# Fused attention, MLP and gated MLP on one core: weight units taken up one step earlier at the start of the middle stage, and set-up work on GpSimd placed behind the first key maxima

## The chip, the cores and the metric

The kernel runs on one core of one Trainium2 chip. The metric is the device time of one execution in microseconds (us). Five engines work side by side, each through its own list of instructions in order: TensorE (PE; its weight loads are shown as PEld), VectorE (DVE), ScalarE (ACT), GpSimd (POOL) and SyncE (SP), which here issues the DMAs. An engine waits only where an instruction needs another engine's result or a buffer that another engine still reads.

## What is computed

The reference, cut to what matters. Everything is fp32.

```python
def _attn_ref(q, k, v):                      # (2, 8, 768, 64) each
    k_sum = k.reshape(B, H, nb, 32, D).max(axis=3)
    v_sum = v.reshape(B, H, nb, 32, D).mean(axis=3)
    scores_l = scale * q @ k.T                # kept where |i - j| < 16
    scores_s = scale * q @ k_sum.T + np.log(32)
    a = softmax(concat[scores_l, scores_s])
    return a @ concat[v, v_sum]

def _moe_ref(x, w_in, w_out):                 # x (1536, 512), d_ff 2048
    h = x @ w_in
    return (h - np.tanh(h)) @ w_out

def _moe2_ref(x, w1, w2, w3, w_out):          # d_ff 1024
    return ((x @ w1) * (x @ w2)) @ w3 @ w_out
```

The attention output, transposed to (1536, 512), goes through `_moe_ref` and then through `_moe2_ref`.

## The kernel before

**Three stages.** The first stage (to about 125 us) is attention: four query tiles at a time, with masks (`masks`), block maxima of the keys (`key_blocks`), softmax, and block means of the values (`value_blocks`, a matmul with the constant rows in `mean`). Beside it TensorE multiplies `w3` by `wo2` (`w34_part`). The middle stage (125 to about 390 us) is `_moe_ref`; the last one is `_moe2_ref`.

**Split products.** An fp32 product is made of three fp32r matmuls: high by high, low by high, high by low (`split_mm`, L187 to L189). So every operand is needed as a high part (a ScalarE cast) and a low part (a GpSimd subtraction of the high part).

**Weight units.** A weight block of 128x512 comes from memory as 64-bit words (`raw`) and is made into fp32 by hand. This is a unit of the class `Weights`: `start` puts one ScalarE instruction (L109); `unit` puts the three VectorE instructions (L112, L114, L116), after which the `raw` buffer is free and SyncE may load the next block (L93); `high` puts the ScalarE cast to `wh` (L144); `low` puts the GpSimd subtraction to `wl` (L151).

**The middle stage.** A loop over n runs over pairs of a feed-forward block f and a token block k. Step n issues the matmuls `hidden(n)` (12, into `ph`), then the pointwise function `curve`, then the matmuls `back(n - 2)` (12, into `x`). `curve(n, ...)` does two things. It ends step n-1: VectorE's conditional copy (L536), then `high()`: the ScalarE cast to `gh` (L531) and the GpSimd subtraction to `gl` (L192). And it begins step n: ScalarE's `u`, `th`, `sq`, `mk` (L544, L545, L550, L551) and VectorE's L552, L553, L554. `back` of a step needs its `gh` and `gl`.

**What sets the order.** The order on each engine is that in which the program text issues the instructions (a manual schedule). In steps below FIRST = 4 the order is `curve`, `start`, `unit`, cast, and `unit` and the cast are there from step LAG = 2 on; from step 4 on it is `start`, cast, and then `curve` with the unit inside it, right behind the conditional copy:

```python
if n < FIRST:
    cur = curve(n, nxt, cur)
wt.start()
...
if LAG <= n < FIRST:
    wt.unit()
if n >= LAG:
    wt.high()
...
if n >= FIRST:
    cur = curve(n, nxt, cur)
wt.low()
```

**The program's start.** GpSimd makes the identity, the diagonal `band`, the rows of `mean`, the three masks, and only then reaches the copy that puts the first key maxima into the key tile (L316 in `key_blocks(0, 2)`). The first `scores` (L347) need that copy.

Of the kernel before, what the change touches and what calls it, by code (L numbers as in the profile page):

```python
# [7 lines left out]
F32 = mybir.dt.float32  # L8
# [4 lines left out]
ALU = mybir.AluOpType  # L13
# [6 lines left out]
P = 128  # L20
NP = H // 2
BLK, WIN = 32, 16
NB = S // BLK
NBR = 3
QT = 64
# [4 lines left out]
CW = QT + NB  # L30
# [11 lines left out]
LAG = 2  # L42
FIRST = 4
# [13 lines left out]
def fused_kernel(tc, qT, kT, vW, w_in, w_out, w1, w2, w3, wo2, out):  # L57
    nc = tc.nc
# [106 lines left out]
    wt = Weights()  # L165
# [25 lines left out]
    def low_part(eng, out, x, high):  # L191
        eng.tensor_tensor(out=out, in0=x, in1=high.bitcast(F32), op=ALU.subtract)  # L192
# [3 lines left out]
    with tc.tile_pool(name="base", bufs=1) as base, \  # L196
# [12 lines left out]
        for hf in range(2):  # L209
            part = band[hf * QT:(hf + 1) * QT, :]  # L210
            nc.gpsimd.affine_select(out=part, in_=part, pattern=[[1, WK]], compare_op=ALU.is_ge,
                                    fill=NEG, base=-1, channel_multiplier=-1)
            nc.gpsimd.affine_select(out=part, in_=part, pattern=[[-1, WK]], compare_op=ALU.is_ge,
                                    fill=NEG, base=2 * WIN - 1, channel_multiplier=1)

        mean = base.tile([P, 6 + BLK], F32, name="mean")
        nc.gpsimd.memset(mean, 0.0)

        def rows(col, a, b):

            nc.gpsimd.memset(col, 1.0 / BLK)
            for base_, step in ((-a, 1), (b - 1, -1)):
                nc.gpsimd.affine_select(out=col, in_=col, pattern=[[0, 1]], compare_op=ALU.is_ge, fill=0.0,
                                        base=base_, channel_multiplier=step)

        rest = base.tile([P, 1], F32, name="mean_rest")
        rows(mean[:, 6:7], WIN, WIN + BLK)
        rows(mean[:, 7:8], WIN + BLK, QT)
        rows(rest, CW, CW + WIN)
        nc.gpsimd.tensor_tensor(out=mean[:, 7:8], in0=mean[:, 7:8], in1=rest, op=ALU.add)  # L230
        masks = []
        for z in range(3):
            mk = base.tile([P, NC], F32, name=f"mask{z}")
            nc.gpsimd.memset(mk[:, BC], LOG_BLK)
            nc.gpsimd.tensor_copy(out=mk[:, :QT], in_=band[:, :QT])
            nc.gpsimd.tensor_copy(out=mk[:, CW:], in_=band[:, QT:])
            if z == 0:
                nc.gpsimd.memset(mk[:, :WIN], NEG)
            if z == 2:
                nc.gpsimd.memset(mk[:, NC - WIN:], NEG)  # L240
            masks.append(mk)

        w34 = [base.tile([P, DM], F32, tag=f"w34_{i}", name=f"w34_{i}") for i in range(NM)]
        xh = [base.tile([P, KC, TB], F32R, name=f"xh_{k}") for k in range(NTB)]
# [31 lines left out]
        with tc.tile_pool(name="p1", bufs=1) as p1, \  # L276
                tc.tile_pool(name="ps1", bufs=1, space=PSUM) as ps1:
            NG = B * NP * NU
            kt, qt, vg, vrow, st, nm, pr, z = ({} for _ in range(8))
# [19 lines left out]
            def key_blocks(n, z):  # L299

                rows = kt[n]
                chunks = rows[:, :NQ * CW].rearrange("p (t w) -> p t w", w=CW)
                if z < 2:
                    if z == 0:
                        hb[n] = p1.tile([P, 4 * NQ + 2], F32, tag="hb", bufs=2, name=f"hb_{n}")
                    t, w = NQ // 2 * z, 2 * NQ
                    nc.vector.tensor_reduce(
                        out=hb[n][:, w * z:w * (z + 1)], axis=AX.X, op=ALU.max,
                        in_=chunks[:, t:t + NQ // 2, :QT].rearrange("p t (i k) -> p t i k", k=WIN))
                else:  # L310
                    nc.vector.tensor_reduce(out=hb[n][:, 4 * NQ:4 * NQ + 1], in_=rows[:, NQ * CW:NQ * CW + WIN],
                                            axis=AX.X, op=ALU.max)
                    pair = [hb[n][:, i:i + 2 * NB].rearrange("p (n two) -> p n two", two=2)[:, :, 0] for i in (1, 2)]
                    kb = p1.tile([P, NB], F32, tag="kb", bufs=2, name=f"kb_{n}")
                    nc.vector.tensor_tensor(out=kb, in0=pair[0], in1=pair[1], op=ALU.max)
                    nc.gpsimd.tensor_copy(out=chunks[:, :, QT:], in_=kb[:, :].unsqueeze(1).to_broadcast([P, NQ, NB]))  # L316
# [23 lines left out]
            def scores(g):  # L340
                n, u = divmod(g, NU)
                ps = ps1.tile([P, TU, NC], F32, tag="s", bufs=2, name=f"s_{g}")
                for i in range(TU):
                    t = u * TU + i
                    for hf in range(2):
                        r = slice(hf * QT, (hf + 1) * QT)
                        mm(out=ps[r, i, :], lhsT=qt[n][r, t * QT:(t + 1) * QT], rhs=kt[n][r, t * CW:t * CW + NC],  # L347
                           start=True, stop=True)
                st[g] = ps
# [33 lines left out]
            def values(g):  # L383
                n, u = divmod(g, NU)
                sb = st[g]
                av = ps1.tile([P, TU * QT + P], F32, tag="av", bufs=1, name=f"av_{g}")
                for i in range(TU):
                    for hf in range(2):
                        r = slice(hf * QT, (hf + 1) * QT)
                        mm(out=av[r, i * QT:(i + 1) * QT], lhsT=vg[n][:NC, u * TU + i, r], rhs=sb[:, i, r],  # L390
                           start=True, stop=True)
                st[g] = av[:, :TU * QT]
                return av[:, TU * QT:]
# [26 lines left out]
            wt.load(2)  # L420
            for i in range(3):
                key_blocks(0, i)
            scores(0)
            n34 = 0
            NN = B * NP
            for g in range(NG + 4):
                n, u = divmod(g, NU)
# [28 lines left out]
                if 0 <= g - 3 < NG:  # L456
                    rest = values(g - 3)
# [51 lines left out]
        def tmp(tag, n, bufs=2, dt=F32):  # L509
            return p2.tile([P, TB], dt, tag=tag, bufs=bufs, name=f"{tag}_{n}")  # L510
# [8 lines left out]
        def hidden(n):  # L519
            f, k = seq[n][:2]  # L520
            ph = bank(n % 3, f"ph_{n}")
            columns(ph, wt.need(("wi", f)), k)
            if k == NTB - 1:
                wt.release(("wi", f))
            return ph

        def curve(n, ph, prev):

            def high():
                gp[n - 1] = tmp("gh", n, LAG + 1, F32R), tmp("gl", n, LAG + 1, F32R)  # L530
                nc.scalar.copy(out=gp[n - 1][0], in_=g)  # L531
                low_part(nc.gpsimd, gp[n - 1][1], g, gp[n - 1][0][:, :])

            if prev is not None:
                mask, t, g = prev
                nc.vector.copy_predicated(out=g, mask=mask[:, :].bitcast(U32), data=t)  # L536
                if n < FIRST:
                    high()
            if n >= FIRST:
                wt.unit()  # L540
            cur = None
            if ph is not None:
                u, sq, t, mask, gn = (tmp(z, n) for z in ("u", "sq", "th", "mk", "g"))
                nc.scalar.activation(out=u, in_=ph, func=AF.Square)  # L544
                nc.scalar.activation(out=t, in_=ph, func=AF.Tanh)  # L545
                cur = mask, t, gn
            if prev is not None and n >= FIRST:
                high()
            if ph is not None:
                nc.scalar.activation(out=sq, in_=u, func=AF.Square, scale=SS, bias=nsb[:])  # L550
                nc.scalar.activation(out=mask, in_=u, func=AF.Relu, bias=numax[:])  # L551
                nc.vector.tensor_tensor(out=gn, in0=ph, in1=u, op=ALU.mult)  # L552
                nc.vector.tensor_tensor(out=t, in0=ph, in1=t, op=ALU.subtract)  # L553
                nc.vector.scalar_tensor_tensor(out=gn, in0=sq, scalar=GAM, in1=gn, op0=ALU.add, op1=ALU.mult)  # L554
            return cur
# [73 lines left out]
        for n in range(NS + LAG):  # L629
            nxt = hidden(n) if n < NS else None  # L630
            if n == NS:
                a = product_a(0, 0)
            if n == NS + 1:
                pb = half("w2", 0, 0)
                w34_split(0)
            if n < FIRST:
                cur = curve(n, nxt, cur)
            wt.start()
            if n == NS + 1:
                prev = 0, 0, product_b(0, 0, a, pb)  # L640
            if LAG <= n < FIRST:
                wt.unit()
            if n >= LAG:
                wt.high()
            closing = len(evac)
            evacuate()
# [3 lines that stand above are left out]
            if not closing:  # L650
                resplit(2)
            if n >= LAG:
                back(n - LAG)
# [108 lines left out]
        for m in range(1, NM):  # L762
# [7 lines left out]
            a = product_a(m, 0)  # L770
# [122 lines left out]
```

## Time and profile before

| | us |
|---|---|
| median of 3 runs | 583.8 (583.33 to 586.09) |
| the profiled execution, its own time | 583.37 |
| its span, first to last instruction | 581.7 |
| PE busy | 565.4 (97% of the span) |
| DVE busy | 462.1 (79%) |
| ACT busy | 339.1 (58%) |
| POOL busy | 280.8 (48%) |

The span is 1.7 us shorter than the time of the same execution. Busy time says who works, not who is waited for: a PE matmul of 512 columns is shown as 0.39 us long, though the next one begins 0.23 us after it, so gaps of PE show only where one is clearly longer than that. The granted TensorE clock is 1.00 in all the stretches used below (2.4 GHz, the upper of its two levels).

### The profile page before, as it was taken

Reading aid. Unit: us, or ns where it says so; the run is one execution under the profiler, and the core shown is the slowest. Engines: PE = TensorE matmul, PEld = TensorE weight load, DVE = VectorE, ACT = ScalarE, POOL = GpSimd, SP = SyncE. Lnnn points to the kernel's source line nnn. Section 1 sums busy time; section 2 is a strip of 40 time slices with the busy share of each in tenths; the row PEclk is TensorE's granted clock in tenths of the full one; section 3 lists DMA queues with packets and bytes.
Section 4 is the critical chain, followed back from the end, with each engine's and each line's share of the span. In section 5 each row is a group of like instructions: output and inputs, shape, how many; then the busy total and the mean of one; then the engine's idle time right before and its main releaser. Section 6 shows DMA issues by size and latency. Waiting matters only on the chain.

```text
span 581.7 us, 9203 instructions
## 1 busy us (share of the span) xinstructions
PE 565.4 (97%) x3240; PEld 458.3 (79%) x3240; DVE 462.1 (79%) x885; ACT 339.1 (58%) x741; POOL 280.8 (48%) x239
## 2 busy tenths in 40 slices
PE   7889999999999999999999999999999999999997
PEld 5677777777688888888888888888887887888885
DVE  4999897766999999679999978999668587778610
ACT  4889887866789776557767667765324322213110
POOL 4556455543465565225555522557735554616320
PEclk9999999999999999999999999999999999999999
DMA  8998875541323323012323101223000100000021
GB/s 318 349 297 303 307 217 186 154 148 37 98 84 109 110 76 106 0 37 73 109 72 109 37 1 51 93 75 110 0 1 0 72 2 1 1 0 2 1 90 54
DMA packets 18526, 56.56 MB, mean 97 GB/s; under 512 B 1968, under 2 KB 4656, under 8 KB 18480
## 3 DMA queue, kind: packets, MB, share of 16 engines
q1 hardware_dynamic: 18480, 55.98, 28.8%
q8 instruction: 25, 0.41, 0.3%
q14 instruction: 21, 0.17, 0.1%
HBM read 51.64 MB, written 3.15 MB: 94 GB/s over the span
## 4 chain that ended last, share of the span: by engine, by line
PE 73%; DVE 12%; issue 5%; ACT 3%; DMA 3%; POOL 2%; SPq 0%; POOLq 0%; DVEq 0%; ACTq 0%
PE x L188 6%; PE x L187 6%; PE x L189 6%; PE ph L187 6%; PE ph L188 6%; PE ph L189 6%; PE p_w L187 4%; PE p_w L189 4%; PE p_w L188 4%; PE o L187 3%; PE o L189 3%; PE o L188 3%; PE w L189 2%; PE w L188 2%; PE w L187 2%
## 5 line engine op out<-in xcount | busy, mean ns | idle before, releaser
L151 POOL TENSOR_TENSOR wl<-dec,wh 128x512 fp32r<-128x512 f32 x72 | 110.7, 1541 | 53.5 <-ACT wh L144 48.3
L192 POOL TENSOR_TENSOR gl<-g,gh 128x512 fp32r<-128x512 f32 x48 | 65.3, 1360 | 133.5 <-ACT gh L531 66.7
L188 PE MATMUL x<-gl,wh 128*128 128x512 f32 x192 | 75.1, 391 | 1.6 <-POOL gl L192 1.6
L187 PE MATMUL x<-gh,wh 128*128 128x512 f32 x192 | 75.0, 390 | 0.1
L187 PE MATMUL ph<-xh,wh 128*128 128x512 f32 x192 | 74.8, 390 | 0.0
L189 PE MATMUL x<-gh,wl 128*128 128x512 f32 x192 | 74.7, 389 | 0.0
L188 PE MATMUL ph<-xl,wh 128*128 128x512 f32 x192 | 74.7, 389 | 0.0
L189 PE MATMUL ph<-xh,wl 128*128 128x512 f32 x192 | 74.7, 389 | 0.0
L116 DVE SCALAR_TENSOR_TENSOR dec<-raw,dec 128x512 uint32<-128x512 uint32 x45 | 60.7, 1348 | 1.5
L544 ACT ACTIVATE u<-ph 128x512 f32<-128x512 f32 x48 | 28.8, 599 | 47.9 <-PE ph L189 47.9
L144 ACT CAST wh<-dec 128x512 fp32r<-128x512 f32 x72 | 44.6, 624 | 17.6 <-DVE dec L116 17.6
L552 DVE TENSOR_TENSOR g<-ph,u 128x512 f32<-128x512 f32 x48 | 32.8, 683 | 21.2 <-ACT th L545 21.1
L188 PEld LDWEIGHTS x<-gl,wh 128*128 128x128 f32 x192 | 36.1, 188 | 10.2 <-POOL gl L192 2.7
L192 POOL TENSOR_TENSOR s_w<-s_w,s_w 128x512 fp32r<-128x512 f32 x16 | 22.9, 1449 | 43.5 <-ACT s_w L723 23.5
L361 ACT ACTIVATE pr<-pr,nm 128x120 f32<-128x120 f32 x96 | 37.1, 391 | 11.4 <-DVE nm L358 11.2
L536 DVE COPY_PREDICATED g<-mk,th 128x512 f32<-128x512 uint32 x48 | 39.7, 826 | 4.2 <-DVE g L554 0.5
L187 PEld LDWEIGHTS x<-gh,wh 128*128 128x128 f32 x192 | 36.0, 188 | 8.5 <-DVE x2a L580 0.5
L187 PEld LDWEIGHTS ph<-xh,wh 128*128 128x128 f32 x192 | 36.1, 188 | 7.6
L189 PEld LDWEIGHTS ph<-xh,wl 128*128 128x128 f32 x192 | 36.1, 188 | 7.5
L188 PEld LDWEIGHTS ph<-xl,wh 128*128 128x128 f32 x192 | 36.0, 188 | 7.4
L189 PEld LDWEIGHTS x<-gh,wl 128*128 128x128 f32 x192 | 36.0, 188 | 7.3
L554 DVE SCALAR_TENSOR_TENSOR g<-sq,g 128x512 f32<-128x512 f32 x48 | 39.3, 820 | 0.7 <-ACT sq L550 0.6
(157 smaller groups left out, 1420.1 us busy)
## 6 DMA issues: line engine op xcount, KB each, us to landing
raw<-w SPq DMA_DIRECT2D x32, 512.0 KB
raw<-w_in SPq DMA_DIRECT2D x16, 512.0 KB
raw<-w_out SPq DMA_DIRECT2D x16, 512.0 KB
vg<-vW SPq DMA_DIRECT2D x8, 768.0 KB
raw<-wo SPq DMA_DIRECT2D x8, 512.0 KB
kt<-kT SPq DMA_DIRECT2D x7, 544.0 KB
qt<-qT SPq DMA_DIRECT2D x7, 384.0 KB
out<-u_out SPq DMA_DIRECT2D x6, 256.0 KB
```

What stands on the lines that cost most here:

```text
L116: lambda tu=tu, su=su, lo=lo: stt(out=tu, in0=lo, scalar=29, in1=su, op0=ALU.logical_shift_right, op1=ALU.bitwise_or)])
L144: nc.scalar.copy(out=h, in_=self.t[n])
L151: nc.gpsimd.tensor_tensor(out=l, in0=self.t[self.n_low], in1=h[:, :].bitcast(F32), op=ALU.subtract)
L187: mm(out=acc, lhsT=lh, rhs=rh, start=start, stop=False)
L188: mm(out=acc, lhsT=lh, rhs=rl, start=False, stop=False)
L189: mm(out=acc, lhsT=ll, rhs=rh, start=False, stop=stop)
L192: eng.tensor_tensor(out=out, in0=x, in1=high.bitcast(F32), op=ALU.subtract)
L361: nc.scalar.activation(out=pr[g][:, i, :], in_=pr[g][:, i, :], func=AF.Exp, scale=-1.0, bias=nm[g][:, i:i + 1], accum_out=z[g][:, i:i + 1])
L536: nc.vector.copy_predicated(out=g, mask=mask[:, :].bitcast(U32), data=t)
L544: nc.scalar.activation(out=u, in_=ph, func=AF.Square)
L552: nc.vector.tensor_tensor(out=gn, in0=ph, in1=u, op=ALU.mult)
L554: nc.vector.scalar_tensor_tensor(out=gn, in0=sq, scalar=GAM, in1=gn, op0=ALU.add, op1=ALU.mult)
```

## The change

It has three parts.

1. At the start, GpSimd makes mask 0 only. Masks 1 and 2 and the rows of `mean` are issued behind the three `key_blocks(0, i)` and ahead of `scores(0)`.
2. In the middle stage `wt.unit()` stands in `curve`, behind the conditional copy, in every step that has a step before it (n from 1 to 48). So steps 1 to 3 have a unit there too, ahead of the curve's own VectorE work, and the unit behind `start` in steps 2 and 3 is gone. Step 49 has none.
3. The ScalarE cast of the weights is issued from step 1 on, not from step 2 on.

```diff
-        mean = base.tile([P, 6 + BLK], F32, name="mean")
...
-        rows(mean[:, 6:7], WIN, WIN + BLK)
...
         masks = []
-        for z in range(3):
+
+        def make_mask(z):
...
+        make_mask(0)
...
             for i in range(3):
                 key_blocks(0, i)
+            make_mask(1)
+            make_mask(2)
+
+            mean = base.tile([P, 6 + BLK], F32, name="mean")
...
+            rows(mean[:, 6:7], WIN, WIN + BLK)
...
             scores(0)
...
                 if n < FIRST:
                     high()
-            if n >= FIRST:
                 wt.unit()
...
-            if LAG <= n < FIRST:
-                wt.unit()
-            if n >= LAG:
+            if n:
                 wt.high()
```

The order on PE and on SP does not change at all. The moves on the other engines are these.

**GpSimd at the start of the program.** In the kernel before, the rows of `mean` (11 instructions, L217 to L230, not shown) come first, then the three masks, then the copy of the first key maxima into the key tile (`kt` from `kb`, L316):

```order
L234 MEMSET mask_102 128x24
L235 COPY mask_102<-band 128x64
L236 COPY mask_102<-band 128x32
L238 MEMSET mask_102 128x16
L234 MEMSET mask_107 128x24
L235 COPY mask_107<-band 128x64
L236 COPY mask_107<-band 128x32
L234 MEMSET mask_111 128x24
L235 COPY mask_111<-band 128x64
L236 COPY mask_111<-band 128x32
L240 MEMSET mask_111 128x16
L316 COPY kt_150<-kb_170 128x12x24
```

In the change (where L219 to L225 are the mask's lines and L303 is that copy):

```order
L213 AFFINE_SELECT band<-band 64x96
L219 MEMSET mask_89 128x24
L220 COPY mask_89<-band 128x64
L221 COPY mask_89<-band 128x32
L223 MEMSET mask_89 128x16
L303 COPY kt_128<-kb_148 128x12x24
L219 MEMSET mask_151 128x24
L220 COPY mask_151<-band 128x64
L221 COPY mask_151<-band 128x32
```

The copy stands behind mask 0 now. Two masks (7 instructions) and the rows of `mean` follow it, ahead of the first softmax product on GpSimd.

**VectorE in steps 0 to 2 of the middle stage.** The numbers behind `g`, `th`, `mk` are the step, those behind `dec` and `raw` the weight unit. Before, from the conditional copy of step 0 on:

```order
L536 COPY_PREDICATED g_0_2009<-mk_0_2008,th_0_2007 128x512
L552 TENSOR_TENSOR g_1_2041<-ph_1_2019,u_1_2037 128x512
L553 TENSOR_TENSOR th_1_2039<-ph_1_2019,th_1_2039 128x512
L554 SCALAR_TENSOR_TENSOR g_1_2041<-sq_1_2038,g_1_2041 128x512
L536 COPY_PREDICATED g_1_2041<-mk_1_2040,th_1_2039 128x512
L552 TENSOR_TENSOR g_2_2073<-ph_2_2051,u_2_2069 128x512
L553 TENSOR_TENSOR th_2_2071<-ph_2_2051,th_2_2071 128x512
L554 SCALAR_TENSOR_TENSOR g_2_2073<-sq_2_2070,g_2_2073 128x512
L112 TENSOR_SCALAR dec_30_1958<-dec_30_1958 128x512
L114 SCALAR_TENSOR_TENSOR dec_30_1958<-raw_30_1868,dec_30_1958 128x512
L116 SCALAR_TENSOR_TENSOR dec_30_1958<-raw_30_1868,dec_30_1958 128x512
L536 COPY_PREDICATED g_2_2073<-mk_2_2072,th_2_2071 128x512
```

In the change (L541 is the conditional copy, L556 to L558 are L552 to L554 of before):

```order
L541 COPY_PREDICATED g_0_2009<-mk_0_2008,th_0_2007 128x512
L112 TENSOR_SCALAR dec_30_1958<-dec_30_1958 128x512
L114 SCALAR_TENSOR_TENSOR dec_30_1958<-raw_30_1868,dec_30_1958 128x512
L116 SCALAR_TENSOR_TENSOR dec_30_1958<-raw_30_1868,dec_30_1958 128x512
L556 TENSOR_TENSOR g_1_2046<-ph_1_2019,u_1_2042 128x512
L557 TENSOR_TENSOR th_1_2044<-ph_1_2019,th_1_2044 128x512
L558 SCALAR_TENSOR_TENSOR g_1_2046<-sq_1_2043,g_1_2046 128x512
L541 COPY_PREDICATED g_1_2046<-mk_1_2045,th_1_2044 128x512
L112 TENSOR_SCALAR dec_31_2017<-dec_31_2017 128x512
L114 SCALAR_TENSOR_TENSOR dec_31_2017<-raw_31_1911,dec_31_2017 128x512
L116 SCALAR_TENSOR_TENSOR dec_31_2017<-raw_31_1911,dec_31_2017 128x512
L556 TENSOR_TENSOR g_2_2087<-ph_2_2060,u_2_2083 128x512
```

Unit 30 moves from behind step 2's curve to behind step 0's copy, and from there on each step has one unit, between the copy and the next curve. Before, units 31 and 32 stand on both sides of step 3's copy; in the change unit 33 is done where before it was unit 32, so the change is one unit ahead until the table of units runs out at step 17.

**ScalarE around the cast `gh` of step 1** (the cast carries the number of the step that issues it, so `gh_2` is of step 1). Before:

```order
L551 ACTIVATE mk_1_2040<-u_1_2037,numax_73 128x512
L109 ACTIVATE dec_32_2049<-raw_32_1916 128x512
L531 CAST gh_2_2065<-g_1_2041 128x512
L544 ACTIVATE u_2_2069<-ph_2_2051 128x512
L545 ACTIVATE th_2_2071<-ph_2_2051 128x512
L550 ACTIVATE sq_2_2070<-u_2_2069,nsb_71 128x512
L551 ACTIVATE mk_2_2072<-u_2_2069,numax_73 128x512
L144 CAST wh_30_2086<-dec_30_1958 128x512
L531 CAST gh_3_2120<-g_2_2073 128x512
```

In the change (L536 is the cast `gh`, L548 to L555 are L544 to L551):

```order
L555 ACTIVATE mk_1_2045<-u_1_2042,numax_73 128x512
L109 ACTIVATE dec_32_2054<-raw_32_1916 128x512
L144 CAST wh_30_2056<-dec_30_1958 128x512
L536 CAST gh_2_2074<-g_1_2046 128x512
L548 ACTIVATE u_2_2083<-ph_2_2060 128x512
L549 ACTIVATE th_2_2085<-ph_2_2060 128x512
L554 ACTIVATE sq_2_2084<-u_2_2083,nsb_71 128x512
L555 ACTIVATE mk_2_2086<-u_2_2083,numax_73 128x512
L109 ACTIVATE dec_33_2095<-raw_33_1956 128x512
L144 CAST wh_31_2097<-dec_31_2017 128x512
L536 CAST gh_3_2131<-g_2_2087 128x512
```

The cast of unit 30 now stands ahead of `gh` of step 1 and not of step 2; GpSimd's subtractions follow in the same order (`gl` of step 0, `wl` of unit 30, `gl` of step 1, and so on). Near the end of the middle stage units 66 to 70 stand one place later on VectorE, ScalarE and GpSimd, since step 49 has no unit.

## Rows read from the trace of the kernel before

**Rows 1.** Busy by stretch: bounds, length, PE, PEld, DVE, ACT, POOL (instructions), clock, DMA share.
```profile
155.00:260.00 105.00, 105.00 (x465) 86.93 (x464) 94.67 (x127) 77.60 (x139) 52.68 (x35) 1.00 0.24 75
```
**Rows 2.** Timeline of PE around its two waits: start, us, engine, line, tiles [idle before].
```profile
133.92 0.39 PE L187 MATMUL x<-gh,wh 128*128 128x512 f32 x1
134.62 0.50 PE L188 MATMUL x<-gl,wh 128*128 128x512 f32 x1 [0.31 <-POOL gl L192]
...
151.25 0.50 PE L187 MATMUL x<-gh,wh 128*128 128x512 f32 x1
153.07 0.50 PE L188 MATMUL x<-gl,wh 128*128 128x512 f32 x1 [1.32 <-POOL gl L192]
```
**Rows 3.** Timeline of the program's start, GpSimd, VectorE and TensorE.
```profile
2.94 0.13 POOL L217 MEMSET mean<- 128x38 f32 x1
...
5.08 0.18 DVE L315 TENSOR_TENSOR kb<-hb 128x24 f32<-128x24 f32 x1
...
6.48 0.42 POOL L316 COPY kt<-kb 128x288 f32<-128x288 f32 x1
...
6.96 0.47 PE L347 MATMUL s<-kt,qt 64*64 64x120 f32 x2 [2.17 <-POOL kt L316]
```
**Rows 4.** Timeline of ScalarE, then of SyncE's issues, at 13 to 17 us.
```profile
13.85 0.66 ACT L109 ACTIVATE bits<-raw 128x512 f32<-128x512 f32 x1 [0.16 <-DMA raw<-w]
14.55 0.26 ACT L332 COPY vr<-pvs 96x128 f32<-96x128 f32 x1
...
14.84 2.35 SPq L337 DMA_DIRECT2D vg<-vr  x3
```
**Rows 5.** Chain of waits that ended last: start, us, what.
```profile
17.23 5.24 DMA raw<-wo
```
**Rows 6.** Timeline of VectorE, steps 0 to 2 of the middle stage.
```profile
131.79 0.75 DVE L536 COPY_PREDICATED g<-mk,th 128x512 f32<-128x512 uint32 x1
134.22 0.69 DVE L552 TENSOR_TENSOR g<-ph,u 128x512 f32<-128x512 f32 x1 [1.67 <-ACT th L545]
136.21 0.76 DVE L536 COPY_PREDICATED g<-mk,th 128x512 f32<-128x512 uint32 x1
...
140.51 0.42 DVE L112 TENSOR_SCALAR dec<-dec 128x512 uint32<-128x512 uint32 x1
140.97 0.69 DVE L114 SCALAR_TENSOR_TENSOR dec<-raw,dec 128x512 uint32<-128x512 uint32 x1
...
142.30 0.76 DVE L536 COPY_PREDICATED g<-mk,th 128x512 f32<-128x512 uint32 x1
```
**Rows 7.** Timeline of GpSimd and of ScalarE in the same steps.
```profile
133.28 1.29 POOL L192 TENSOR_TENSOR gl<-g,gh 128x512 fp32r<-128x512 f32 x1 [4.49 <-ACT gh L531]
...
135.30 0.66 ACT L109 ACTIVATE dec<-raw 128x512 f32<-128x512 f32 x1
...
142.42 0.62 ACT L144 CAST wh<-dec 128x512 fp32r<-128x512 f32 x1 [2.59 <-DVE dec L116]
```
**Rows 8.** Timeline of VectorE and GpSimd around step 6's copy and unit 35.
```profile
162.82 0.68 DVE L554 SCALAR_TENSOR_TENSOR g<-sq,g 128x512 f32<-128x512 f32 x1
162.82 1.83 POOL L151 TENSOR_TENSOR wl<-dec,wh 128x512 fp32r<-128x512 f32 x1
163.60 1.68 DVE L536 COPY_PREDICATED g<-mk,th 128x512 f32<-128x512 uint32 x1
...
165.62 0.69 DVE L114 SCALAR_TENSOR_TENSOR dec<-raw,dec 128x512 uint32<-128x512 uint32 x1
166.07 1.41 POOL L192 TENSOR_TENSOR gl<-g,gh 128x512 fp32r<-128x512 f32 x1 [1.42 <-issue]
166.35 1.68 DVE L116 SCALAR_TENSOR_TENSOR dec<-raw,dec 128x512 uint32<-128x512 uint32 x1
```
**Rows 9.** Timeline of ScalarE in step 6, of VectorE in the last stage.
```profile
157.84 2.04 ACT L578 COPY x2a<-x 128x512 f32<-128x512 f32 x4
...
417.51 0.69 DVE L610 TENSOR_TENSOR u_a<-u_a,w 128x512 f32<-128x512 f32 x1 [2.15 <-PE w L189]
```

More of the change, by code (lines that the diff above doesn't have):

```diff
@@ L214, in fused_kernel @@
                                     fill=NEG, base=2 * WIN - 1, channel_multiplier=1)
-        mean = base.tile([P, 6 + BLK], F32, name="mean")
[L217 to L226, printed above, removed]
-        rows(mean[:, 6:7], WIN, WIN + BLK)
-        rows(mean[:, 7:8], WIN + BLK, QT)
-        rows(rest, CW, CW + WIN)
-        nc.gpsimd.tensor_tensor(out=mean[:, 7:8], in0=mean[:, 7:8], in1=rest, op=ALU.add)
         masks = []
-        for z in range(3):
+        def make_mask(z):
             mk = base.tile([P, NC], F32, name=f"mask{z}")
@@ L422, in fused_kernel, with rows @@
                 key_blocks(0, i)
+            make_mask(1)
+            make_mask(2)
+            mean = base.tile([P, 6 + BLK], F32, name="mean")
+            nc.gpsimd.memset(mean, 0.0)
+            def rows(col, a, b):
+                nc.gpsimd.memset(col, 1.0 / BLK)
+                for base_, step in ((-a, 1), (b - 1, -1)):
+                    nc.gpsimd.affine_select(out=col, in_=col, pattern=[[0, 1]], compare_op=ALU.is_ge, fill=0.0,
+                                            base=base_, channel_multiplier=step)
+            rest = base.tile([P, 1], F32, name="mean_rest")
+            rows(mean[:, 6:7], WIN, WIN + BLK)
+            rows(mean[:, 7:8], WIN + BLK, QT)
+            rows(rest, CW, CW + WIN)
+            nc.gpsimd.tensor_tensor(out=mean[:, 7:8], in0=mean[:, 7:8], in1=rest, op=ALU.add)
             scores(0)
```

## The prediction

> **What bounds the kernel now.** I read the busy time by stretch first, then the timeline of TensorE for places where two matmuls start further apart than usual, then the chain of waits and the timelines of the other engines around those places. From 155 to 260 us TensorE has no gap: 465 matmuls in 105.00 us, one every 0.226 us [rows 1]. A step of the middle stage is 24 of them, 5.43 us. So what shifts TensorE at the start of this stage is kept to the end, and what leaves TensorE alone is worth nothing.
>
> In the first steps TensorE waits twice, both times for the low part `gl` of the curve [rows 2]. In step 0 the second matmul of `back` starts 0.70 us behind the first, in step 3 it is 1.82 us. Less the usual 0.226 that is 0.47 and 1.59, together 2.06 us. This is what the middle part of the change can take away; slow restarts around these waits add about 0.4 at most.
>
> At the program's start the first scores wait for GpSimd's copy of the key maxima. VectorE has the maxima at 5.26 (5.08 + 0.18); GpSimd reaches the copy at 6.48, since it has worked at `mean` and masks without a pause from 2.94 on [rows 3]. The chain of waits begins there.
>
> **Part 1, the start.** Ahead of the copy 4 of the 22 instructions that began at 2.94 are left, so GpSimd waits for VectorE instead, and the copy begins at about 5.31: 1.17 us earlier, and with it scores and softmax. The 18 others run behind the copy until about 9 us; masks 1 and 2 are done 1 us after it, ahead of the softmax that needs them (2 us behind the copy), the rows of `mean` 4 us before the value means that need them at about 12.
>
> How much of the 1.17 lives on? ScalarE's L109 of the second unit waits at 13.85 for the landing of its DMA [rows 4]. That DMA was issued before any computing and gets no earlier. Behind it on ScalarE stands the copy L332, which SyncE waits for with three DMAs (14.84) and all that is queued behind them, of which the chain's next link is the load at 17.23 [rows 4, 5]. L332 starts at 14.55 now and could start about 14.41, when L109 lets it (0.66 long, the next one may start some 0.1 before its end). So the gain is bounded by 0.14 on this path; VectorE, which comes up to a microsecond early, then waits for the same loads. Bounds: 0 and 1.17. I take **-0.15**, the path that the chain goes along.
>
> **Part 2, the unit behind the copy.** The three instructions of a unit take 1.79 us from the first to the next instruction (140.51 to 142.30). After step 0's copy VectorE idles 1.67 us [rows 6]. By durations alone the unit of step 1 fits and is free, as do the later ones, and `gl` of steps 2 and 3 would come earlier. But the rows show that GpSimd and VectorE get in each other's way. At 165.62 L114 starts; `gl` arrives at 166.07 and takes 1.41 and not 1.29 us; L116 behind them takes 1.68 and not 0.69 [rows 8]. And `wl` arriving with L554 (162.82) takes 1.83, and the copy L536 behind takes 1.68 and not 0.76 [rows 8]. So L114, L116, L554 and L536 (both inputs in SBUF) can't run while GpSimd's subtraction does: whichever comes first holds the other up. From these rows VectorE's instruction holds GpSimd for 0.55 us (1.83 - 1.29 is 0.54), and VectorE loses 0.99 at L116 or 0.92 at L536.
>
> Now the replay. `gl` comes 1.49 us behind the start of its copy (131.79 to 133.28) [rows 6, 7]. In the change L114 of unit 30 starts at about 132.91 (0.66 for the copy, 0.46 for L112), so `gl` of step 0 arrives 0.37 into it: the collision of 166.07. It ends 0.15 later than now (TensorE's first wait grows to 0.6), and L552 of step 1 starts at 135.2, not at 134.22. The cast of unit 30 stands behind L109 (135.30) on ScalarE, so it runs from 135.84 to 136.46 (0.62 long) [rows 7], and `wl` arrives at 136.53. L554 starts 0.78 before the copy, at 136.43: the collision of 162.82. The copy of step 1 is due at 137.2, 1 us late, and takes 0.92 more; `gl` of step 1 arrives at 139.6 (as the next unit's L114 runs) and ends at 141.06.
>
> From there each step without another wait has copy 0.66, unit 1.79, L552 to copy 1.99 (134.22 to 136.21) [rows 6], and both collisions, 0.99 and 0.92: 6.35 us, against TensorE's 5.43. So `gl` of steps 2 and 3 end at 147.4 and 153.75, and TensorE waits 0.7 to 0.8 in each of steps 1 to 3. Its second matmul of step 3's `back` starts at 153.8, where it starts at 153.07 now [rows 2]: **+0.7**. Three short waits take the place of one long one.
>
> From step 4 on the cast stands ahead of the curve, `wl` comes right behind `gl`, and the second collision is mostly gone, as now. But in step 6 four copies (2.04 us) stand on ScalarE behind a weight cast [rows 9]. VectorE is 2.5 us later in the curve by then and one unit ahead: the cast waits for its unit until 159.7, the copies end at about 162, and `gl` of step 5 ends at 165.3, when TensorE has been there for 0.55. With the slow restart (0.11): **+0.65**. Bounds of this term: 0, if the copies come in time, and 1.3, if the same is met again four steps later.
>
> By the Trainium skill (SBUF — State Buffer, "SBUF: two separate sides") the shared port pair is held for the whole instruction, 0.69 and not 0.55 us, and the loser starts only after that. An estimate from it: 0.26 more per collision, two per step, 1.6 us more by step 3, so 586.6; the lengths in rows 8 contradict that (L116 there starts its 0.69 before `gl` has ended), and I go by the rows.
>
> **Part 3, the rest.** The cast from step 1 on is counted above. The table of units runs out a step earlier: VectorE has 1.8 us less in step 18, TensorE has no gap there, nothing. Near the end of the stage units 66 to 70 are put together a place later. They are needed 10 us and more after that; where one more stands ahead of L610, VectorE idles 2.15 us now [rows 9], more than 1.79. Nothing; without that cover it would be 1.8 - 2.15, still nothing, up to 0.6 with one collision.
>
> **The sum.** -0.15 + 0.7 + 0.65 = +1.2 us on the profiled execution's 583.4, so 584.6. The median of the runs, 583.8, lies 0.4 above that execution; on it the forecast is **585.0**.
>
> **The rivals.**
> (a) *The collisions don't happen* in these steps, since `gl` or `wl` falls between the pairs. For it: the unit fits the idle time of 1.67 almost exactly, and small shifts decide. Against it: the copy sets off both the unit and `gl`, so their distance is fixed, and the pattern of 166.07 comes back in most of the later steps. Then the wait of 1.59 goes with its restarts, 2.0 in all: 583.8 - 2.0 - 0.15 = 581.7; with the whole 1.17 at the start 580.6.
> (b) *The start keeps all of its 1.17*, as SyncE's DMAs get out earlier; the collisions stay: 583.8 - 1.17 + 1.35 = 584.0. Against it stands the landing that ScalarE waits for.
> (c) *Slower: steps of 6.35 don't end at step 4.* If at step 4 and behind it `wl` still arrives between L554 and the copy, each step costs 0.92 more than TensorE's 5.43. It decides from the fourth such step: 0.7 + 4 x 0.92 - 0.15 is 4.2, so 588. For it: VectorE is only just fast enough there (4.44 + 0.99 is TensorE's 5.43). Against: the new order on ScalarE from step 4 on.
> (d) *The gain and the waits cancel*, the 0.65 of step 6 not coming and the start giving a little more: 583.8 to 584.3.
>
> **How the numbers follow.** Forecast 0.48, (a) 0.22 (of which 0.06 with the whole start), (b) 0.08, (c) 0.08, (d) 0.14. A measurement of this kernel tells 0.5% from no change, 2.9 us: faster is below 580.9, slower above 586.7. Faster: the low end of (a), 0.07. Slower: (c) and a little of the forecast's upper bound, 0.09. Same: 0.84. The range goes from 581.2, which takes in (a) with the small gain at the start, to 587.0 (the forecast with its upper bound, 585.65, the longer hold of the port and the spread of the runs shown, up to 586.1).
>
> **What would show it.** Right: the copy of the key maxima at about 5.3, L332 at about 14.4; TensorE's second matmul of `back` waiting in each of steps 0 to 3, 0.5 to 0.8 us; L116 and the conditional copy 1.68 long in each of these steps; step 3's at 153.6 or so (less what the start gave). Wrong: L116 of unit 30 at 0.69, no wait in steps 1 to 3, and `back` of step 3 at 151.0.

## The result and the profile after

The changed kernel takes 592.37 us in the median of 4 runs (591.82 to 593.87), the kernel before 584.43 beside it (4 runs): the ratio is 1.0137, 95% interval 1.0113 to 1.0162. It is 8 us slower; the forecast was 585.0 with 587.0 as its upper end. The profiled execution took 591.82 us, its span is 590.1 (before 581.7).

The page of the changed kernel, span and busy time: TensorE is busy 8.6 us longer with the same 3240 matmuls.

```profile
span 590.1 us, 9205 instructions
...
PE 574.0 (97%) x3240; PEld 460.2 (78%) x3240; DVE 470.9 (80%) x885; ACT 338.3 (57%) x741; POOL 281.9 (48%) x239
```

**The first four waits are those of the forecast.** Timeline of TensorE in the changed kernel at `back` of steps 0, 1, 3 and 4 (start, us, engine, line, tiles [idle before]); it answers to [rows 2]:

```profile
135.42 0.40 PE L187 MATMUL x<-gh,wh 128*128 128x512 f32 x1
136.12 0.50 PE L188 MATMUL x<-gl,wh 128*128 128x512 f32 x1 [0.30 <-POOL gl L192]
...
141.52 0.40 PE L187 MATMUL x<-gh,wh 128*128 128x512 f32 x1
142.41 0.50 PE L188 MATMUL x<-gl,wh 128*128 128x512 f32 x1 [0.49 <-POOL gl L192]
...
154.10 0.40 PE L187 MATMUL x<-gh,wh 128*128 128x512 f32 x1
154.99 0.50 PE L188 MATMUL x<-gl,wh 128*128 128x512 f32 x1 [0.49 <-POOL gl L192]
...
160.88 0.40 PE L189 MATMUL x<-gh,wl 128*128 128x512 f32 x1
162.09 0.50 PE L187 MATMUL x<-gh,wh 128*128 128x512 f32 x1 [0.81 <-ACT x2a L582]
```

Four waits of 0.5 to 0.7 us (start to start less the usual 0.226) stand where there were one of 0.47 and one of 1.59, and a fifth of 0.98 is new: there TensorE waits for the copies of `x2a` (L582). From the first `ph` matmul to the last of the program I took the starts of neighbouring matmuls that lie more than 0.26 us apart; what they have above 0.2267 sums to 4.84 us, before to 4.17. So the waits explain 0.67 us of the 8.4 by which the span grew.

**The rest is a slower TensorE that waits for nothing.** Busy time by stretch, 165 to 255 us, where neither kernel has a wait (columns as in [rows 1]). The kernel before:

```profile
165.00:255.00 90.00, 90.00 (x399) 74.53 (x398) 80.54 (x109) 64.83 (x115) 45.12 (x30) 1.00 0.22 71
```

The changed kernel, with the same full clock:

```profile
165.00:255.00 90.00, 90.00 (x393) 73.32 (x391) 79.79 (x106) 63.10 (x112) 46.05 (x30) 1.00 0.22 71
```

Six matmuls fewer in 90 us. The timeline of TensorE in the changed kernel shows which they are (12 matmuls into `ph`, of which four are shown, then the first into `x`):

```profile
258.20 0.40 PE L187 MATMUL ph<-xh,wh 128*128 128x512 f32 x1
...
260.06 0.40 PE L189 MATMUL ph<-xh,wl 128*128 128x512 f32 x1
260.30 0.39 PE L187 MATMUL ph<-xh,wh 128*128 128x512 f32 x1
260.52 0.40 PE L188 MATMUL ph<-xl,wh 128*128 128x512 f32 x1
...
260.99 0.39 PE L187 MATMUL x<-gh,wh 128*128 128x512 f32 x1
```

The 12 `ph` matmuls take 2.79 us, 232.5 ns each (start to start), in this step as in the 46 others without a restart among them; in the kernel before it is 2.72. Of the 12 matmuls into `x` behind them the first three still take 231 to 233 ns in the mean of all steps and the other nine 227, as all of them do before. Over all matmuls from the first `ph` on, what is above 226.7 ns without being a wait sums to 8.41 us, before to 1.98: **+6.43**. The changed kernel's first `ph` starts 1.32 us later (126.95 for 125.63). 1.32 + 0.67 + 6.43 is the 8.4.

What differs for these matmuls is where `xh` and `xl` lie. They are the moving operands of the `ph` matmuls (`rhs`, the first tile behind the arrow); the second tile, here the weights, is the stationary operand (`lhsT`), which the PEld rows load. The change moves not only the instructions on masks 1, 2 and `mean` but the declarations of their tiles, which now stand behind `xl` in the pool `base`. So `w34`, `xh` and `xl` lie 1,152 bytes per partition lower: in the compiled programs `xh` starts at 35488 before and at 34336 after. The remainder of these addresses by 512 is 160 before and 32 after; the weights, `gh` and `gl` have 160 in both.

### The profile page after: what moved, and what is told of

Same layout as the page of the kernel before. It is cut to its first block, busy times and chain, and to the rows that moved or that the text cites. A ratio compares the mean times of both kernels' runs of the same rounds, so it can differ in the third digit from the quotient of the medians.

```text
span 590.1 us, 9205 instructions
## 1 busy us (share of the span) xinstructions
PE 574.0 (97%) x3240; PEld 460.2 (78%) x3240; DVE 470.9 (80%) x885; ACT 338.3 (57%) x741; POOL 281.9 (48%) x239
## 4 chain that ended last, share of the span: by engine, by line
PE 84%; DVE 8%; issue 3%; DMA 2%; ACT 1%; POOL 0%; SPq 0%; DVEq 0%; ACTq 0%
PE x L187 7%; PE x L188 7%; PE x L189 7%; PE ph L187 7%; PE ph L189 7%; PE ph L188 7%; PE p_w L187 4%; PE p_w L189 4%; PE p_w L188 4%; PE o L187 4%; PE o L189 4%; PE o L188 4%; PE w L189 3%; PE w L188 3%; PE w L187 3%
## 5 line engine op out<-in xcount | busy, mean ns | idle before, releaser
L116 DVE SCALAR_TENSOR_TENSOR dec<-raw,dec 128x512 uint32<-128x512 uint32 x45 | 60.9, 1354 | 1.5
L548 ACT ACTIVATE u<-ph 128x512 f32<-128x512 f32 x48 | 28.8, 599 | 55.6 <-PE ph L189 55.6
L541 DVE COPY_PREDICATED g<-mk,th 128x512 f32<-128x512 uint32 x48 | 46.4, 967 | 4.0
L556 DVE TENSOR_TENSOR g<-ph,u 128x512 f32<-128x512 f32 x48 | 32.8, 683 | 20.2 <-ACT th L549 20.0
L536 ACT CAST gh<-g 128x512 fp32r<-128x512 f32 x48 | 29.9, 623 | 17.6 <-DVE g L541 17.3
```

The lines of the kernel that those rows point to most:

```text
L116: lambda tu=tu, su=su, lo=lo: stt(out=tu, in0=lo, scalar=29, in1=su, op0=ALU.logical_shift_right, op1=ALU.bitwise_or)])
```

## The experiments

Theory: the pace of a matmul depends on where its two operands lie. Rival: the new order of the instructions slows TensorE. Beside each time stands the kernel before on the same chip (584.17, 585.23 and 584.16 us in three groups); the ratios are taken over all runs and need not be those of two medians. Since the start of the program varies from execution to execution (below), I also give the time from the first `ph` matmul to the last matmul of the profiled execution: 452.06 us before, 459.17 in the changed kernel.

### Old order or old places

e1, the changed kernel with the old places:

```diff
+        mean = base.tile([P, 6 + BLK], F32, name="mean")
+        rest = base.tile([P, 1], F32, name="mean_rest")
+        mask_tiles = [base.tile([P, NC], F32, name=f"mask{z}") for z in range(3)]
         masks = []
...
-            mk = base.tile([P, NC], F32, name=f"mask{z}")
+            mk = mask_tiles[z]
```

> The changed kernel, instruction for instruction, with one edit: mean, mean_rest and the three masks are declared in `base` where they were before, so that w34, xh and xl lie 1,152 bytes per partition higher again, at their old addresses. Placement theory: the matmuls on xh and xl go every 227 ns again instead of 232 (mean of the stretch 200 to 390 us: 226.7 instead of 230.3 ns), and about 5 us come back: 587 us, 2.5 over before. Order theory (the moved units, casts and masks themselves slow TensorE, whatever the addresses): 592 us, and 232 ns stay. In both, the waits of the middle stage's first steps stay as they are in the changed kernel (0.69, 0.89, 0.89, 0.89, 1.21 us gaps).

Measured: 585.88 us, ratio 1.0029 (1.0009 to 1.0050). The row of its stretch has the old count:

```profile
165.00:255.00 90.00, 90.00 (x399) 74.53 (x398) 79.74 (x106) 64.86 (x115) 44.79 (x31) 1.00 0.22 71
```

e2, the kernel before with the new places (`w34`, `xh`, `xl` declared between mask 0 and the other tiles, no instruction moved):

> The kernel before, instruction for instruction, with one edit: mask 1, mask 2, mean and mean_rest are declared behind xl in `base`, so that w34, xh and xl get the addresses that they have in the changed kernel. Placement theory: 232 ns for the matmuls on xh and xl from 126 us on, and some 5 to 6 us more: 590 us. Order theory: 584.4 us and 227 ns, as before.

Measured: 589.37 us, ratio 1.0088 (1.0062 to 1.0114), 5.2 us more without a single instruction moved. Its row:

```profile
165.00:255.00 90.00, 90.00 (x392) 73.37 (x391) 79.33 (x107) 62.80 (x114) 44.52 (x31) 1.00 0.24 72
```

From the first `ph` on e1 takes 453.78 us (+1.72), e2 457.52 (+5.46). The order theory has fallen: the places make the pace.

### Which places

```diff
+        base.tile([P, A // 4], F32, name="pad_a")
         w34 = [base.tile([P, DM], F32, tag=f"w34_{i}", name=f"w34_{i}") for i in range(NM)]
...
         xl = [base.tile([P, KC, TB], F32R, name=f"xl_{k}") for k in range(NTB)]
+        base.tile([P, B // 4], F32, name="pad_b")
```

e5 has A = 320 and no B, e6 A = B = 256, e7 A = 32 and B = 480; e8 is the changed kernel with A = 448, B = 384.

> The kernel before with 320 unused bytes per partition declared ahead of w34 in `base`. Now every operand of the split matmuls, the weights' as well as the moving ones, the last stage's too, has the remainder 480 by 512 (before: 160, but x2a, t2 and a few weights of the last stage 480). Relation theory (a matmul is slower where the addresses of its moving and its stationary operand differ by 512): 227 ns in the whole program; the 1.6 us that before loses behind 455 us by slower matmuls (229.8 ns for 226.7, 526 of them) goes too: 582.6 us. Absolute theory (a remainder of 160 is what is fast): 232 ns from 126 us on and 590 us. Rival (something else than the remainder, such as the distance to a certain tile): anything from 582 to 590.

> The kernel before with 256 unused bytes ahead of w34 and 256 behind xl: w34, xh and xl move by 256 bytes and nothing else changes its remainder by 512 (xh, xl 416, weights 160). If the relation goes by 512: 230 to 232 ns on xh and xl, about 589 us. If it goes by 256: 227 ns and 584.2 us, as before.

> The kernel before with 32 unused bytes ahead of w34 and 480 behind xl: xh and xl have the remainder 192, the weights 160. If any difference counts: 230 to 232 ns on xh and xl, about 589 us, as with a difference of 128. If it only counts from 64 or 128 bytes up: 227 ns and 584.2 us.

> The changed kernel with 448 unused bytes ahead of w34 and 384 behind xl: every operand of the split matmuls has the remainder 480. Relation theory: the 8.4 us that the changed kernel loses between 126 us and the end by matmuls slower than 226.7 ns go, but for a few tenths; the waits of the first steps grow by some 0.5 us as in the run with the old places, since TensorE comes to them sooner: 584.4 us, 1.8 over the kernel before at the same remainder. Absolute theory: 592 us.

Measured, with the mean start-to-start time of the middle stage's matmuls (waits left out), and what all matmuls from the first `ph` on lose above 226.7 ns:

| | remainder of xh, xl / of weights | ns per matmul | lost, us | first `ph` to end, us | median, us | ratio to before |
|---|---|---|---|---|---|---|
| before | 160 / 160 | 226.8 | 1.98 | 452.06 | | |
| e5 | 480 / 480 | 226.9 | 0.31 | 450.49 | 583.54 | 0.9993 (0.9967 to 1.0019) |
| e6 | 416 / 160 | 226.8 | 1.91 | 451.93 | 585.26 | 1.0003 (0.9981 to 1.0026) |
| e7 | 192 / 160 | 231.7 | 10.46 | 459.36 | 592.92 | 1.0137 (1.0099 to 1.0176) |
| after | 32 / 160 | 230.4 | 8.41 | 459.17 | 592.37 | 1.0137 (1.0113 to 1.0162) |
| e8 | 480 / 480 | 226.9 | 0.48 | 452.43 | 585.20 | 1.0002 (0.9982 to 1.0022) |

The row of e7, the slowest, and then that of e6:

```profile
165.00:255.00 90.00, 90.00 (x390) 72.91 (x389) 81.42 (x109) 63.84 (x116) 47.23 (x31) 1.00 0.24 77
```

```profile
165.00:255.00 90.00, 90.00 (x399) 74.53 (x398) 80.55 (x108) 64.99 (x116) 45.75 (x31) 1.00 0.24 76
```

A remainder of 480 everywhere is as fast as 160 (e5), so no single remainder is the fast one. A difference of 256 between the two operands costs nothing (e6), which I had left open; differences of 32 (e7) and 128 (after, e2) cost 3.6 to 4.9 ns in the mean over `ph` and `x`. So in these runs the stage keeps its pace where the starts of a matmul's moving and stationary operand differ by a multiple of 256 bytes. e7 cost 3.9 us more than expected; there the `x` matmuls, whose own operands agree, slow down too (to 229.8 ns). It is the first seven of each twelve, as it is the first three in the changed kernel, so a slow matmul also holds up those behind it.

Whether the stationary operand that counts is the matmul's own or that of the next one, which PEld loads beside it, this table can't tell, since all weights of the stage lie alike. The last stage of the kernel before speaks for its own: ten matmuls whose operands agree stand there ahead of one whose operands don't, and that one starts 226 ns later. Why the difference matters wasn't tried.

The kernel before has such pairs itself: in the last stage, where `t2` and some weights and products lie at 480 and the others at 160. Row of 23 us out of its last 120 matmuls into `o`, without a wait, and then that of e5:

```profile
552.00:575.00 23.00, 23.00 (x101) 18.68 (x100) 3.41 (x5) 2.90 (x5) 4.30 (x4) 1.00 0.21 80
```

```profile
551.00:574.00 23.00, 23.00 (x103) 19.06 (x102) 3.11 (x5) 2.91 (x5) 3.98 (x3) 1.00 0.22 80
```

Of the matmuls that start in the first row 37 have operands that don't agree; the 62 others go every 231.0 ns too, held up by those around them. e5 gains 1.56 us from its first `ph` on in the profiled execution. Its runs alone don't prove it (the interval includes 1).

### The parts of the change, at the old places

e3 has the start alone, e4 the middle stage alone (the hunks of the diff, with e1's declarations in e3).

> The first part of the change alone (masks 1 and 2 and the rows of the means made behind the first keys' maxima), at the old addresses, with the middle stage of before. As predicted: the first scores start 1.36 us earlier than before (5.60 for 6.96), and nearly all of it is lost at the weight units, 584.3 us. Clock theory (the granted clock rises 4 us later, at 14.5 instead of 10.5 us, because of the other order of TensorE's first work): the middle stage starts 1.3 us later than before, 585.7 us. If the late rise was chance in one profiled execution, the clock rises at 10.5 here or elsewhere at random, and the time is 583.1 to 584.4 us.

> The second part of the change alone (the unit in the curve of every step, the cast behind it from step 1 on), start and addresses of before. Collision theory, as predicted: gaps of 0.7 to 0.9 us in the first four steps in place of one of 1.6 and one of 0.6, and one of 1.2 at step 5, together 1.35 us more than before: 585.8 us. Rival (no collisions of VectorE with GpSimd decide it): 583 us, the 1.6-us gap gone and nothing in its place. Order theory for TensorE's pace: 232 ns on xh and xl and 590 us; placement theory: 227 ns.

Measured: e3 585.27 us, ratio 1.0001 (0.9981 to 1.0022); e4 586.00, ratio 1.0038 (1.0017 to 1.0060). From the first `ph` on e3 takes 452.00 us (as before), e4 453.71 (+1.65): the middle part costs 1.65 us where 1.35 were forecast, and 227 ns stay.

e4 also bears on the late start of the changed kernel. It has the start of before, and still its first `ph` starts at 130.04, for in this execution TensorE's early matmuls were slow for longer. Timeline of TensorE in e4, then in e5, with the same instructions:

```profile
10.29 3.35 PE L411 MATMUL busy<-ident 128*128 128x128 f32 x8
13.57 1.87 PE L347 MATMUL s<-kt,qt 64*64 64x120 f32 x16
```

```profile
10.29 2.43 PE L412 MATMUL busy<-ident 128*128 128x128 f32 x8
12.65 1.04 PE L348 MATMUL s<-kt,qt 64*64 64x120 f32 x16
```

The changed kernel's profiled execution shows the slow figures as well, and so its copy `vr` waits:

```profile
8.99 3.35 PE L398 MATMUL busy<-ident 128*128 128x128 f32 x8
12.28 1.87 PE L334 MATMUL s<-kt,qt 64*64 64x120 f32 x16
```

```profile
15.41 0.26 ACT L319 COPY vr<-pvs 96x128 f32<-96x128 f32 x1 [1.70 <-PE pvs L314]
```

With the new start both happen, as the same row of e3 and then that of e1 shows:

```profile
12.82 1.87 PE L337 MATMUL s<-kt,qt 64*64 64x120 f32 x16
```

```profile
11.63 1.04 PE L337 MATMUL s<-kt,qt 64*64 64x120 f32 x16
```

Over all 13 profiled executions these 16 matmuls take 1.86 or 1.87 us in 4 of 8 with the old start and in 3 of 5 with the new one, and 1.04 in all others. The first `ph` starts between 125.2 and 130.0 us with the old start (mean 127.9) and between 125.6 and 128.9 with the new one (mean 127.1); where the 16 matmuls take 1.87 it is 127.0 to 130.0, where they take 1.04 it is 125.2 to 127.5. e3 alone would have spoken for its clock theory, with the slow figure and the first `ph` at 127.87. Over all executions that theory has fallen: the +1.32 lies within the scatter and is not of the new order.

The rows of these first stretches print a granted clock of 1.00, so that the clock makes the slow pace is read from the matmuls; the first record of a full clock in the traces stands at 8.9 to 11.5 us where the 16 matmuls take 1.04 and at 14.5 to 18.8 where they take 1.87. The Trainium skill (TensorE: Matmul & The Clock Gate, Part 1) says that the moment at which the clock rises does not follow the start of the kernel alone. These records agree, with a wider scatter than the half microsecond that the Trainium skill gives there.

### The waits of the first steps

e10 tries the collisions, e9 and e11 the wait of 1.59 us in the kernel before; all have every operand at 480. e10, on e8:

```diff
                 nc.scalar.copy(out=gp[n - 1][0], in_=g)
-                low_part(nc.gpsimd, gp[n - 1][1], g, gp[n - 1][0][:, :])
+                if n < FIRST and wt.n_dve < len(wt.t):
+                    wt.dve(2)
+                low_part(nc.vector if n < FIRST else nc.gpsimd, gp[n - 1][1], g, gp[n - 1][0][:, :])
```

> The changed kernel at 480 (as in the run of that name) with the subtraction gl of steps 1 to 3 on VectorE, between the second and the third instruction of the unit, instead of on GpSimd. Collision theory (VectorE's third instruction, L116, takes 1.66 instead of 0.69 us because GpSimd's subtraction runs then): L116 takes 0.69 in these three steps, gl is ready some 0.5 us sooner, the steps get shorter than 6.28 us, and the three waits of 0.62 to 0.70 us at 135 to 148 us fall to 0.2 or less: about 1.5 us off. Rival (the chain copy, cast, subtraction is what is late, with or without a collision): L116 is short, but the waits stay over 0.5 us.

Measured: 583.84 us, ratio 0.9992 (0.9972 to 1.0011); from the first `ph` on 451.21 us, 1.22 under e8. Timeline of VectorE in e10, steps 0 to 2:

```profile
136.71 0.68 DVE L192 TENSOR_TENSOR gl<-g,gh 128x512 fp32r<-128x512 f32 x1
137.31 0.68 DVE L116 SCALAR_TENSOR_TENSOR dec<-raw,dec 128x512 uint32<-128x512 uint32 x1
...
139.90 1.77 DVE L545 COPY_PREDICATED g<-mk,th 128x512 f32<-128x512 uint32 x1
...
143.22 0.68 DVE L116 SCALAR_TENSOR_TENSOR dec<-raw,dec 128x512 uint32<-128x512 uint32 x1
```

And GpSimd, idle until then:

```profile
139.77 1.29 POOL L151 TENSOR_TENSOR wl<-dec,wh 128x512 fp32r<-128x512 f32 x1 [7.75 <-ACT wh L144]
```

L116 is 0.68 us again as soon as GpSimd does nothing beside it, so the collision is its cause. The copy still collides with `wl` (1.77). The three waits (0.64, 0.71 and 0.70 us in e8) become 0.08, 0.33 and 0.35, so only the first falls as far as the collision theory asked, and step 3's wait grows to 0.85. How much of the waits was the collision's this run can't tell: on VectorE `gl` itself takes 0.68 us and not 1.44, which shortens the chain with or without a collision.

e9 and e11, on e5 (e11 without the two lines on the unit):

```diff
-                if n < FIRST:
+                if n <= FIRST:
                     high()
-            if n >= FIRST:
+            if n > FIRST:
                 wt.unit()
...
-            if prev is not None and n >= FIRST:
+            if prev is not None and n > FIRST:
                 high()
```

> The kernel before with every operand at 480 and, in step 4, no weight unit ahead of the curve and the cast of gh right behind the copy (as in the steps before it) instead of behind that step's square and tanh. The wait of 1.6 us at 150 us in the kernel before is of the second unit in a row (L112 to L116 twice between two curves, the second one's L114 1.67 us long beside GpSimd's wl) and of the late cast: with both gone the gl of that step should be ready 1.1 us sooner or more, the wait fall to 0.3 us or less, and the time to 1.3 to 1.5 us under the run with all at 480 alone. Rival: the weights made one unit later are then late for a later step, and the wait only moves: no gain.

> As the run without the second unit in step 4, but with the unit left there: only the cast of gh in step 4 stands right behind the copy. If the late cast alone makes the wait of 1.6 us: 0.3 us or less is left. If the second unit does: 1.2 us or more is left, since VectorE's L114 and GpSimd's subtractions still run at the same time.

Measured: e9 583.38 us, ratio 0.9979 (0.9961 to 0.9996); e11 585.10, ratio 0.9999 (0.9978 to 1.0021). TensorE at this wait in e9, then in e11:

```profile
154.83 0.39 PE L187 MATMUL x<-gh,wh 128*128 128x512 f32 x1
155.55 0.50 PE L188 MATMUL x<-gl,wh 128*128 128x512 f32 x1 [0.33 <-POOL gl L192]
```

```profile
155.21 0.39 PE L187 MATMUL x<-gh,wh 128*128 128x512 f32 x1
156.46 0.50 PE L188 MATMUL x<-gl,wh 128*128 128x512 f32 x1 [0.86 <-POOL gl L192]
```

The wait of 1.6 us falls to 1.02 by the early cast (e11) and to 0.49 where the unit is gone as well (e9), so both had a share; the 0.3 or less that was expected of e9 did not come. In e11 the gain is lost at once, since `back` then waits 1.05 us for the copies of `x2a`. In e9 most of it comes back later, as the rival had it: the table of units runs out one step later, and its last unit now stands in the step in which VectorE adds to `x2a`. Timeline of VectorE in e9, with no such unit in e5:

```profile
233.38 0.41 DVE L112 TENSOR_SCALAR dec<-dec 128x512 uint32<-128x512 uint32 x1
...
237.94 2.47 DVE L581 TENSOR_TENSOR x2a<-x,x2a 128x512 f32<-128x512 f32 x4
```

And TensorE there:

```profile
237.76 0.39 PE L189 MATMUL x<-gh,wl 128*128 128x512 f32 x1
238.66 0.50 PE L187 MATMUL x<-gh,wh 128*128 128x512 f32 x1 [0.52 <-DVE x2a L581]
```

From the first `ph` on e9 takes 450.41 us, e5 450.49 and e11 451.06: the waits' gain is gone, the places' gain stays. e9 is the one version whose interval lies below 1, but it is one of eleven intervals, and in the profiled executions it is only 0.08 us under e5, whose interval includes 1. That e9 is faster than the kernel before is likely and not shown.

## Why the prediction was wrong

**The step that failed** is in the part on the bound: the gapless TensorE's 0.226 us per matmul, read from the kernel before, is taken for both kernels, so that only what shifts it at the start of the stage counts. The pace itself changed, by some 6 ns in the middle stage's `ph` matmuls, 1 in those into `x` and 3 in the mean of the last stage: 6.43 us that no term of the sum holds. I followed every moved instruction and not the moved declarations, which stand in the diff as plainly. The middle stage of the kernel before could not show the price, since all pairs agree there; the last stage had it in sight, with 229.0 ns per matmul in the mean and 226.8 in the middle stage. The sentence at the start that an engine waits only for a result or a buffer is too narrow for the same reason: these matmuls wait for neither.

**Part 2 was right in its mechanism, and in its second term by another path.** At the old places (e1) the first `ph` starts at 125.64, as before (125.63), so its timeline of VectorE can be laid beside the replay of the forecast:

```profile
132.89 0.69 DVE L114 SCALAR_TENSOR_TENSOR dec<-raw,dec 128x512 uint32<-128x512 uint32 x1
133.62 1.66 DVE L116 SCALAR_TENSOR_TENSOR dec<-raw,dec 128x512 uint32<-128x512 uint32 x1
135.20 0.68 DVE L557 TENSOR_TENSOR g<-ph,u 128x512 f32<-128x512 f32 x1
...
136.40 0.68 DVE L559 SCALAR_TENSOR_TENSOR g<-sq,g 128x512 f32<-128x512 f32 x1
137.18 1.67 DVE L542 COPY_PREDICATED g<-mk,th 128x512 f32<-128x512 uint32 x1
```

Forecast were 132.91 for L114, 135.2 for the curve, 136.43 for its third instruction and 137.2 for the copy, with both collisions, which answer to [rows 8]. Step 3's second matmul of `back` starts at 153.65 (forecast 153.8): +0.58 for the +0.7. The second term came as 1.16 (1.05 and the slow restart) and not 0.65, by a shorter way: TensorE waits for the four copies of `x2a` themselves, one step earlier, not for the `gl` behind them. Together 1.72 from the first `ph` on, where 1.35 was forecast; that the sum comes so near is in part luck, as one term is too large and the other too small. In the changed kernel it is only 0.67, since its slower `ph` matmuls come later to the same waits; in e2, with the order of before, the waits shrink likewise, from 4.17 to 3.08 us.

**Part 1** (-0.15) can't be told from nothing: ratio 1.0001 in e3. The copy of the key maxima starts at 5.12 in the changed kernel, near the forecast 5.31; [rows 4] would have let `vr` start at 14.41, and e1 has it at 14.26.

**Part 3** (nothing) held: no new wait in the changed kernel behind step 6.

**The rivals.** (a) fell, the collisions happen. (b), 1.17 us kept at the start, would be a ratio of 0.9980 in e3, just outside its interval (from 0.9981), so it is unlikely and not excluded with any margin. (c) had the right side and the wrong mechanism: the steps of 6.28 us do end at step 4. (d) fell as well, since the waits cost 1.72 us at the old places (e1) and its interval excludes 1.

## What to carry to other kernels

When a change moves the declaration of a tile, list the addresses of all tiles behind it, and compare them for the two operands of each matmul: here a difference that is not a multiple of 256 bytes cost 2% of TensorE's pace. Compare the pace of a stretch without waits before looking for waits; if the same matmuls go slower there under the same granted clock, look at the places of their operands before the order of the instructions. And a unit of work taken out of a crowded step must go somewhere: look at the step that gets it.

## What was not expected of the hardware

- An fp32r matmul of 512 columns goes every 226.7 ns or, in the mean, every 232, by the start addresses of its operands alone, and matmuls right behind a slow one are slowed with it (e2 and the table above).
- The early matmuls run at half pace for a time that differs between executions of the same instructions (16 matmuls in 1.87 or 1.04 us), and in some executions once more later. The row of e4 for this stretch shows a granted clock of 0.50, the lower of the two levels, with TensorE busy for 2.92 of 3.30 us:

```profile
36.40:39.70 3.30, 2.92 (x41) 2.32 (x41) 1.47 (x10) 0.07 (x1) 0.00 (x0) 0.50 1.03 411
```

With the slow early matmuls the first `ph` came up to 4.8 us later (125.2 to 130.0), which is why effects under 2 us need the timeline beside the runs.
